# GpSimd makes the top bits of four weight halves, the first two in-projections begin in parts, and the first 30 steps get another order

## The chip, the cores and the metric

The kernel runs on one core of a Trainium2 chip. The metric is the device time of one execution in microseconds (us); lower is better. TensorE (PE) multiplies matrices, VectorE (DVE), ScalarE (ACT) and GpSimd (POOL) work elementwise, and SyncE (SP) issues nearly all DMAs. Each engine takes its instructions in the order of the program.

## The reference, cut to what matters

Chunked attention with a short window and 8 memory keys, and behind it a projection with a rational function between its two matrices:

```python
for c in range(nc):                     # 24 chunks of 32 queries, 4 batches x 8 heads, head_dim 64
    k_full = concat([mem_k, k[l_start:r_end]])        # v alike: 8 memory keys and up to 56 of the window
    a = softmax(scale * q_c @ k_full.T)
    out[c] = a @ v_full
x = out laid out as [3072, 512]
h = x @ w_in                            # w_in [512, 2048], float64 in memory
P = a0 + a1*h + a2*h**2 + a3*h**3
Q = 1 + |b0|*|h| + |b1|*h**2
return ((P / (Q + 1e-6)) @ w_out).astype(float32)     # w_out [2048, 512], float64
```

The two weight matrices are float64; the kernel gets them as pairs of 32-bit words and makes float32 of them itself.

## The kernel before, in words

The 3072 tokens are 8 blocks of 384. Attention of a block is done in 4 units (i, p): block i, head pair p. Block by block, 16 tiles j of 128 hidden features are worked through: the in-projection `g1` (12 matmuls of 384 columns: 4 slices `ct` of the contraction, each as high x high, low x high, high x low of an fp32r split), the rational function (the `chain_...` functions), and the out-projection `g2` (9 matmuls of 512 columns). One pair (i, j) is a step; `order` numbers them from 0 to 127.

In-projection n needs the four slices of x of its block, that is all four attention units, and the converted weights of its tile. Its result lies in one of two PSUM buffers `h`, which is free again for n + 2 when `chain_above` of n is done.

The first 30 steps (`HAND`) and the attention of blocks 0 to 2 are written out by hand in `SEQ`, a list of tokens; every token issues its instructions on its engines in that order, and so the string sets the order on each engine, SP's queue of DMAs too. From step 30 on a loop sets the order. The tokens, with what the prediction calls them:

- `q00`, `v00`: load of a unit's queries and keys (2 DMAs of 212 KB) and of its values (2 of 195 KB). `w`: load of one half of a weight tile (512 KB). Which half comes next is in `ORDER` (i5 is the in-half of tile 5, o5 the out-half); the tokens A, B, H, L take the halves in the same order.
- `b` scores (24 matmuls), `m` maximum and difference on DVE, `x` exponential on ACT, `c` three transposes, `k` copy of the result on ACT, `d` values (24 matmuls), `n` division on DVE, `e` three transposes back, `h` the high part of x on ACT, `l` the low part of x. For units in `XL_POOL`, `h` makes one more copy on ACT (line 432) and `l` runs on POOL (line 438), for the others on DVE (line 442).
- Conversion of a weight half: `A` (ACT, line 172) puts the rebiased high word into PSUM, `B` (DVE, two instructions, lines 177 and 178) shifts that by 3 and ors in the top 3 bits of the low word, `H` (ACT) rounds to the fp32r high part, `L` (POOL, line 190) subtracts.
- `g`: the next in-projection; `s` and `i` (ACT), `p` (POOL), `j` (DVE, `chain_above`), `t` (ACT), `r` (DVE, `chain_ratio`), `u` and `y` (POOL): its chain; `o`: the next out-projection. The prediction numbers these from 0.
- `W`: one filler transpose of the identity. `begin` issues `WARM` of them first, behind the clearing of the tiles into which q and v are loaded (`CLEAR`: tile, unit, and the engine for each half of it: v DVE, a ACT, p POOL).
- `M`: block 0's x is stored to memory. `E`: an output is moved out.

SBUF tiles are shared through slots (`QK_SLOTS`, `RAW_SLOTS`, `V_SLOTS`). q10 goes to the tile of q00 and waits until the scores b00 have read it, as q12 waits for b02; v02 lies in slot 10, v10 goes to the tile of v00.

Of the kernel before, what the change touches and what calls it, by code (L numbers as in the profile page):

```python
# [12 lines left out]
F32 = mybir.dt.float32  # L13
# [3 lines left out]
ALU = mybir.AluOpType  # L17
# [9 lines left out]
SIGN_STEP = 2.0 ** 32  # L27
W_SCALE = 2.0 ** 8
SPLIT = 10
XL_POOL = [(0, 0), (0, 1), (0, 2), (0, 3), (1, 0), (1, 1), (1, 2), (1, 3), (2, 0)]  # L30
WARM = 14
CLEAR = [("qk", 2, "va"), ("qk", 3, "pa"), ("qk", 0, "vp"), ("qk", 1, "pa"), ("v", 3, "pv"), ("v", 2, "av"), ("v", 1, "va"), ("v", 0, "ap")]
HAND = 30
BLOCKWISE = 3
BASES = {3: [30, 32, 35, 37], 4: [40, 42, 46, 50]}
# [8 lines left out]
SEQ = """
w q00 q03 q01 b00 v03 b03 m00 q02 W b01 m03 A B x00 x03 W c03 k03 w m01 W W d03 q10 b02 v01 x01 Y A c01 n03 e03 m02 w
v00 H w k01 c00 b10 h03 B x02 v02 m10 l03 d01 k00 c02 A q13 k02 x10 n01 q11 P H d00 L e01 B L w A v10 c10 d02 n00 h01
k10 H w l01 B w q12 e00 b13 n02 L b11 e02 m13 h00 A l00 m11 W d10 w h02 l02 x11 H A B c11 g k11 q21 b12 H L n10 L e10
v11 A g x13 b21 B c13 w s i B A m12 p H t j B s w d11 x12 r L c12 H g k13 v12 v13 m21 q20 n11 i w h10 j e11 k12 A L p
B t l10 s u h11 w y i p g l11 r A s w H d13 t u j i H L o n13 p x21 w B r d12 w e13 L h13 g n12 b20 y w l13 j H w A B
s L t A m20 o i B H g A H x20 u j e12 r h12 p y L L l12 v20 o s u g A B B q22 t w y c20 H r H c21 i k21 L p k20 q23 j  # L50
A A o u B t s B r g b23 L H y H i p s A L j u v21 i y m23 B M x23 o L t w g H b22 d21 j r p n21 s o A m22 L g B e21
c23 u y p i t w h21 r u s p j l21 i o k23 t g y j A H r A L u B y s g i v23 B t o H p w L r x22 u j y s H d20 d23 o
n20 t A r i w p t B j g r L s w i o u w y p g A E t o u j B w e20 s p v22 i r t j y g h20 s r H l20 p u i g j A o B
n23 g L c22 t e23 s w u p y k22 i r o t y j r s p H L H i g h23 u w A o j l23 d22 y u B o t s i A p g y r o t L j u y
s H r p n22 i t e22 B h22 u g j A H r s l22 i p L A w B A y t j B r o w u g g s i p t A L s y j o u p y H i B g r j s
t i p r H o g o u L j y B s t g E w r u y i p L o j g o s t u y H w p r L i j A B t u s p g r i H o s t j y L u A i w
r j p H L t y g B A B s p H o r u i y H g o s p u j o t g r y L u i j t y o s r i j g p o L q30 v30
"""
# [15 lines left out]
def attn_moe(ctx, tc, qk, vm, w, ab, out):  # L74
    nc = tc.nc
    P = 128
# [3 lines left out]
    TB = out.shape[0] // NBLK  # L80
# [4 lines left out]
    NCT = DM // P  # L85
# [11 lines left out]
    ps_h = ctx.enter_context(tc.tile_pool(name="ps_h", bufs=2, space=bass.MemoryType.PSUM))  # L97
# [44 lines left out]
    def half(t, kind):  # L142
        return t[:, :2 * DM] if kind == "in" else t[:, 2 * DM:]
# [50 lines left out]
    xh = {i: x_hi[i % 2] for i in range(NBLK)}  # L194
    xl = {i: x_lo[i % 2] for i in range(NBLK)}
# [559 lines left out]
```

## Time and profile before

| | us |
|---|---|
| median of 3 runs | 619.98 (618.28 to 620.85) |
| the profiled execution's own time | 619.44 |
| its span (first to last instruction) | 617.6 |
| TensorE busy | 599.1 (97%) |
| VectorE busy | 495.3 (80%) |
| ScalarE busy | 435.8 (71%) |
| GpSimd busy | 433.0 (70%) |

Busy times are shares of the span; the matmuls are pipelined, so that a group of them ends a little after the next has begun. A line of the timeline gives start, duration, engine, source line, operation, output and inputs, how many instructions are merged, and in brackets the idle time of the engine before it with what ended it. The trace of the profiled execution is what all sums below are made against; its own time is 0.54 us under the median.

### The profile page before, as it was taken

What the parts mean: (1) busy time and instruction counts of PE and PEld (TensorE: products, weight loads), DVE (VectorE), ACT (ScalarE), POOL (GpSimd) and SP (SyncE); (2) the same over time, 40 slices, a digit from 0 to 9 for tenths busy, and PEclk for the clock granted to TensorE, in tenths of its full rate; (3) what the DMA queues carried; (4) which work ended last, traced back from release to release, by engine and by line L of the source; (5) the groups of instructions that cost most, each with busy time, mean ns of one, the idle gap of its engine ahead of it and who ended that gap; (6) DMA issues with size and microseconds to landing.
All of it is one profiled execution on the core that took longest, in us unless ns stands there. A gap on an engine that the chain in (4) does not pass through costs nothing.

```text
span 617.6 us, 14151 instructions
## 1 busy us (share of the span) xinstructions
PE 599.1 (97%) x5275; PEld 528.8 (86%) x5275; DVE 495.3 (80%) x991; ACT 435.8 (71%) x822; POOL 433.0 (70%) x459
## 2 busy tenths in 40 slices
PE   6689999999999999999999999999999999999997
PEld 5568889899888888988889898888889888989996
DVE  6899998898867979788778787777878777666674
ACT  5799888798756766666667766676676766676674
POOL 2579987879966667766767676766767676776773
PEclk9999999999999999999999999999999999999999
DMA  7989437103023574342221322242122310010001
GB/s 259 359 280 360 162 110 254 48 1 146 2 83 86 177 212 146 119 133 81 82 81 38 116 68 75 81 133 82 36 62 68 101 27 14 14 51 2 0 1 51
DMA packets 42788, 64.81 MB, mean 105 GB/s; under 512 B 25696, under 2 KB 25696, under 8 KB 42336
## 3 DMA queue, kind: packets, MB, share of 16 engines
q1 hardware_dynamic: 41856, 60.61, 30.6%
q10 hardware_dynamic: 576, 1.74, 0.9%
q0 software_dynamic: 288, 1.57, 0.8%
q8 instruction: 41, 0.67, 0.4%
q14 instruction: 27, 0.22, 0.1%
HBM read 46.60 MB, written 9.44 MB: 91 GB/s over the span
## 4 chain that ended last, share of the span: by engine, by line
PE 53%; issue 18%; POOL 15%; DMA 5%; DVE 4%; ACT 2%; SPq 1%; POOLq 0%; DVEq 0%
PE o L477 25%; PE h L462 24%; POOL glo L551 6%; POOL ghi L544 6%; DMA qk<-in_qk_dram 2%; DMA w_raw<-in_w_dram 2%; POOL x_lo L440 1%; PE pairs L300 1%; POOL cy L518 1%; PE pairs L323 1%; SPq L125 1%; DMA v_main<-in_vm_dram 1%; DVE stage L177 1%; PE pa L347 1%; DVE ct L528 1%
## 5 line engine op out<-in xcount | busy, mean ns | idle before, releaser
L462 PE MATMUL h<-x_hi,w_hl 128*128 128x384 f32 x1024 | 265.1, 339 | 0.9 <-DVE ct L528 0.5
L477 PE MATMUL o<-w_hl,ghi 128*128 128x512 f32 x768 | 239.6, 393 | 0.0
L518 POOL TENSOR_TENSOR cy<-cy,ha 128x384 f32<-128x384 f32 x128 | 130.4, 1019 | 140.8 <-ACT cy L514 135.5
L462 PEld LDWEIGHTS h<-x_hi,w_hl 128*128 128x128 f32 x1024 | 185.3, 188 | 12.6 <-DVE ct L528 2.1
L462 PE MATMUL h<-x_lo,w_hl 128*128 128x384 f32 x512 | 172.5, 337 | 0.0
L477 PEld LDWEIGHTS o<-w_hl,ghi 128*128 128x128 f32 x768 | 141.8, 188 | 20.8 <-issue 0.8
L477 PE MATMUL o<-w_hl,glo 128*128 128x512 f32 x384 | 150.9, 393 | 0.0
L551 POOL TENSOR_TENSOR glo<-ct,ghi 128x384 fp32r<-128x384 f32 x127 | 129.1, 1017 | 8.9
L513 ACT ACTIVATE ha<-h 128x384 f32<-128x384 f32 x128 | 62.9, 492 | 91.7 <-PE h L462 89.4
L527 DVE TENSOR_TENSOR ct<-ct,h 128x384 f32<-128x384 f32 x128 | 70.1, 548 | 57.6 <-ACT ct L523 57.4
L544 POOL TENSOR_TENSOR ghi<-ct,zero 128x384 fp32r<-128x384 f32 x127 | 105.4, 830 | 3.8 <-DVE ct L539 2.7
L537 DVE SCALAR_TENSOR_TENSOR ct<-ct,par,cr 128x384 f32<-128x384 f32 x128 | 78.5, 613 | 33.9 <-ACT cr L533 30.9
L532 ACT ACTIVATE cr<-cy 128x384 f32<-128x384 f32 x128 | 63.2, 494 | 58.3 <-POOL cy L518 54.1
L462 PEld LDWEIGHTS h<-x_lo,w_hl 128*128 128x128 f32 x512 | 96.0, 188 | 0.0
L514 ACT ACTIVATE cy<-ha,bab 128x384 f32<-128x384 f32 x128 | 90.9, 710 | 4.5 <-DVE cr L538 0.3
L477 PEld LDWEIGHTS o<-w_hl,glo 128*128 128x128 f32 x384 | 72.0, 187 | 20.2 <-POOL glo L551 0.8
L523 ACT ACTIVATE ct<-h,par 128x384 f32<-128x384 f32 x128 | 84.1, 657 | 0.1
L528 DVE SCALAR_TENSOR_TENSOR ct<-ct,par,h 128x384 f32<-128x384 f32 x128 | 78.7, 615 | 4.5
L539 DVE SCALAR_TENSOR_TENSOR ct<-cr,ct 128x384 f32<-128x384 f32 x128 | 71.4, 558 | 4.4
L538 DVE SCALAR_TENSOR_TENSOR cr<-cy,cr 128x384 f32<-128x384 f32 x128 | 71.1, 556 | 0.4
L533 ACT ACTIVATE cr<-cr 128x384 f32<-128x384 f32 x128 | 60.8, 475 | 4.0
L190 POOL TENSOR_TENSOR w_hl<-w_raw,w_hl 128x512 fp32r<-128x512 f32 x32 | 42.1, 1316 | 6.8 <-ACT w_hl L185 6.1
(69 smaller groups left out, 406.9 us busy)
## 6 DMA issues: line engine op xcount, KB each, us to landing
w_raw<-in_w_dram SPq DMA_DIRECT2D x26, 512.0 KB, 7.0
v_main<-in_vm_dram SPq DMA_DIRECT2D x20, 390.0 KB, 4.7
qk_pairs<-in_qk_dram SPq DMA_DIRECT2D x16, 424.0 KB, 4.2
out_dram<-stage SPq DMA_DIRECT2D x24, 256.0 KB, 3.8
qk<-in_qk_dram SPq DMA_DIRECT2D x24, 212.0 KB, 4.8
v_main<-in_vm_dram SPq DMA_DIRECT2D x20, 195.0 KB, 6.0
eT<-blocks SPq DMA_DIRECT2D x80, 48.0 KB, 2.0
xf<-blocks SPq DMA_DIRECT2D x80, 48.0 KB, 2.0
```

The source lines that it names most:

```text
L462: pin(nc.tensor.matmul(h[:, :TB], lhsT=wt[:, cols], rhs=xt[i][:, ct, :], start=m == 0, stop=m == last))
L477: ins = nc.tensor.matmul(o, lhsT=gt[:, cols], rhs=wt, start=begin and m == 0, stop=end and m == 2)
L514: pin(nc.scalar.activation(c["y"], c["ha"], AF.Identity, scale=B1, bias=B0))
L518: pin(nc.gpsimd.tensor_tensor(c["y"], c["y"], c.pop("ha"), op=ALU.mult))
L523: pin(nc.scalar.activation(c["t"], c["h"], AF.Identity, scale=A3, bias=A2))
L527: pin(nc.vector.tensor_tensor(t, t, h, op=ALU.mult))
L528: pin(nc.vector.scalar_tensor_tensor(t, t, A1, h, op0=ALU.add, op1=ALU.mult))
L537: pin(nc.vector.scalar_tensor_tensor(t, t, A0, r, op0=ALU.add, op1=ALU.mult))
L538: pin(nc.vector.scalar_tensor_tensor(r, yy, QC, r, op0=ALU.add, op1=ALU.mult))
L539: pin(nc.vector.scalar_tensor_tensor(t, r, 2.0, t, op0=ALU.subtract, op1=ALU.mult, reverse0=True))
L544: pin(nc.gpsimd.tensor_tensor(ghi, chain[z]["t"], zero.broadcast_to([P, TB]), op=ALU.add))
L551: pin(engine.tensor_tensor(glo, chain.pop(z)["t"], gh[z].bitcast(F32), op=ALU.subtract))
```

## The change

The order string `SEQ` is replaced as a whole. Beside it:

```diff
-XL_POOL = [(0, 0), ..., (1, 3), (2, 0)]
+XL_POOL = [(0, 0), ..., (1, 3), (2, 1), (2, 2), (2, 3)]
-WARM = 14
-CLEAR = [("qk", 2, "va"), ("qk", 3, "pa"), ("qk", 0, "vp"), ("qk", 1, "pa"), ("v", 3, "pv"), ("v", 2, "av"), ("v", 1, "va"), ("v", 0, "ap")]
+WARM = 28
+CLEAR = [("qk", 0, "pv"), ("qk", 2, "pp"), ("v", 0, "va"), ("v", 3, "aa"), ("v", 2, "va"), ("qk", 3, "pp"), ("qk", 1, "pv"), ("v", 1, "pp")]
-ORDER = "i0 o0 i1 o1 i4 i2 i3 o3 i5 o2 i6 o4 ..."
+ORDER = "i0 i1 i2 i4 o0 i3 o1 o2 i5 i6 o3 i7 ..."
 SEQ = """
-w q00 q03 q01 b00 v03 b03 m00 q02 W b01 m03 A B x00 x03 W c03 k03 w m01 W W d03 q10 b02 v01 x01 Y A c01 n03 e03 m02 w
-v00 H w k01 c00 b10 h03 B x02 v02 m10 l03 d01 k00 c02 A q13 k02 x10 n01 q11 P H d00 L e01 B L w A v10 c10 d02 n00 h01
-k10 H w l01 B w q12 e00 b13 n02 L b11 e02 m13 h00 A l00 m11 W d10 w h02 l02 x11 H A B c11 g k11 q21 b12 H L n10 L e10
-v11 A g x13 b21 B c13 w s i B A m12 p H t j B s w d11 x12 r L c12 H g k13 v12 v13 m21 q20 n11 i w h10 j e11 k12 A L p
...
+w A q00 q03 b03 v03 q01 b00 w m03 m00 R x03 c03 x00 q10 B k03 b01 A d03 R m01 b10 q02 c00 n03 m10 B e03 x01 v01 v00
+c01 H k00 b02 Y L k01 h03 m02 d01 x10 l03 n01 x02 d00 H w e01 q11 c10 n00 A R q13 h01 c02 L e00 v02 w B l01 k02 k10
+b13 h00 H l00 b11 w d02 P m13 m11 f01 A R x11 v10 A f00 n02 c11 e02 k11 B L h02 d10 w w f10 q12 H A w l02 f11 f02 B
+x13 n10 B g A B b12 c13 H q21 v11 f12 e10 b21 w L s p m12 i A v12 t H k13 j H g s B L i p r d11 w x12 v13 g n11 j A t
...
-RAW_SLOTS = [9, 6, 9, 7, 8, 11, 13, 14, 12, 10, 12, 14, 16, 11, 15, 16]
+RAW_SLOTS = [8, 7, 5, 10, 9, 12, 13, 14, 11, 10, 11, 14, 16, 15, 15, 16]

+TOP_BITS = 4
+    def w_tops(key):                                   # token R
+        low, high = words(key)
+        tops = half(raws[key[1]], key[0]).bitcast(mybir.dt.uint16).rearrange("p (f four) -> p f four", four=4)[:, :, 1]
+        pin(nc.gpsimd.tensor_scalar(low, tops, 2.0 ** -13, 7.0, op0=ALU.mult, op1=ALU.min))
     def w_bits(key):                                   # token B
+        if done["B"] < TOP_BITS:
+            pin(nc.vector.scalar_tensor_tensor(low, fi, 3, low, op0=ALU.logical_shift_left, op1=ALU.bitwise_or))
+            return
         pin(nc.vector.tensor_scalar(fi, fi, 3, None, op0=ALU.logical_shift_left))
         pin(nc.vector.scalar_tensor_tensor(low, low, 29, fi, op0=ALU.logical_shift_right, op1=ALU.bitwise_or))
-    def g1(n):
+    def g1(n, only=None):
+        if n not in ahead:
+            ahead[n] = list(range(NCT))
+            hps[n] = ps_h.tile([P, 512], F32, name="h", tag="h")
+        left, h = ahead[n], hps[n]
+        for ct in [only] if only is not None else list(left):
+            terms = ((w_hi, xh), (w_lo, xh), (w_hi, xl))
+            for m, (wt, xt) in enumerate(terms):
+                pin(nc.tensor.matmul(..., start=len(left) == NCT and m == 0, stop=len(left) == 1 and m == len(terms) - 1))
+            left.remove(ct)
...
+        elif kind == "f":                              # token f01: step 0, slice ct 1
+            g1(i, p)
```

A token `f` does three matmuls, those of one slice, of in-projection 0 or 1; a later `g` does the slices that are left. The rounding of the top bits is new: they are scaled and converted, where they were shifted.

## Rows read from the trace of the kernel before

**Rows 1.** Windows: length, busy (count) of PE, PEld, DVE, ACT, POOL, clock, DMA share, GB/s.
```profile
0.00:5.97 5.97, 3.25 (x14) 2.88 (x15) 3.01 (x5) 5.22 (x8) 4.24 (x14) 1.00 0.63 204
5.97:32.35 26.38, 17.65 (x335) 13.30 (x336) 21.05 (x49) 15.81 (x34) 9.88 (x9) 1.00 0.95 338
32.35:44.70 12.35, 10.96 (x120) 9.10 (x120) 11.72 (x25) 11.30 (x25) 8.59 (x9) 1.00 0.81 270
44.70:60.00 15.30, 15.18 (x136) 12.66 (x137) 14.65 (x30) 14.99 (x30) 14.51 (x15) 1.00 0.97 340
60.00:80.00 20.00, 19.21 (x158) 15.80 (x157) 19.30 (x38) 16.93 (x33) 18.06 (x18) 1.00 0.57 208
80.00:617.60 537.60, 532.82 (x4516) 475.07 (x4514) 425.61 (x848) 371.53 (x697) 377.70 (x397) 1.00 0.26 78
```

**Rows 2.** Windows of line 598 alone (fillers): length, PE, PEld, clock, DMA, GB/s.
```profile
0.00:32.35 32.35, 4.56 (x19) 3.52 (x19) 1.00 0.89 313
```

**Rows 3.** Timeline of PE: the fillers, the first scores, and the waits behind them.
```profile
2.21 3.25 PE L598 MATMUL warm<-ident 128*128 128x128 f32 x14 [2.21 <-POOL ident masks.py:199]
5.97 0.86 PE L347 MATMUL pa<-qk 128*32 128x128 f32 x24 [0.51 <-DMA qk<-in_qk_dram]
7.94 0.86 PE L347 MATMUL pa<-qk 128*32 128x128 f32 x24 [1.10 <-DMA qk<-in_qk_dram]
...
22.34 0.87 PE L402 MATMUL pa<-v_first,eT 128*32 128x130 f32 x24 [0.58 <-DMA v_first<-in_vm_dram]
...
32.35 0.86 PE L347 MATMUL pa<-qk 128*32 128x128 f32 x24 [0.97 <-DMA qk<-in_qk_dram]
...
41.32 0.52 PE L425 MATMUL pa<-ident,xt 128*128 128x128 f32 x3 [0.88 <-DVE xt L415]
42.34 0.62 PE L462 MATMUL h<-x_hi,w_hl 128*128 128x384 f32 x2 [0.50 <-DVE ct L528]
```

**Rows 4.** Tile qk: clears on POOL, count, ns min/median/max, first and last start.
```profile
L217 POOL MEMSET qk<- x5: 485/485/486, 0.9 to 4.3; 128x464 f32 x5
```

**Rows 5.** Timeline of SP: DMA issues q00 q03 q01, and q10.
```profile
1.88 3.75 SPq L125 DMA_DIRECT2D qk<-in_qk_dram  x6
...
8.91 1.12 SPq L125 DMA_DIRECT2D qk<-in_qk_dram  x2
```

**Rows 6.** Timeline of DVE: the first maximum, both instructions of B, waits.
```profile
6.93 0.09 DVE L357 MEMSET pa<- 32x32 f32 x1 [2.62 <-PE pa L347]
...
10.80 0.69 DVE L178 SCALAR_TENSOR_TENSOR w_raw<-w_raw,stage 128x512 uint32<-128x512 uint32 x1
...
19.64 0.70 DVE L177 TENSOR_SCALAR stage<-stage 128x512 uint32<-128x512 uint32 x1 [0.86 <-ACT stage L172]
...
22.70 0.73 DVE L178 SCALAR_TENSOR_TENSOR w_raw<-w_raw,stage 128x512 uint32<-128x512 uint32 x1
```

**Rows 7.** Waits of DVE, 5 to 90 us: total, times, longest.
```profile
DVE pa L357 <- PE pa L347: 3.3, 2, 2.6
DVE stage L177 <- ACT stage L172: 1.9, 3, 0.9
```

**Rows 8.** DMA issues up to 32.35 us: count, KB each, median us to landing.
```profile
w_raw<-in_w_dram SPq DMA_DIRECT2D x10, 512.0 KB, 6.5
qk<-in_qk_dram SPq DMA_DIRECT2D x18, 212.0 KB, 4.8
```

**Rows 9.** Chain of waits, from 32 us: start, duration, a whole in-projection.
```profile
33.70 2.10 PE h L462 x12
```

**Rows 10.** Timeline of POOL: the first work behind the clears, and one L.
```profile
16.82 1.01 POOL L438 TENSOR_TENSOR x_lo<-xf,x_hi 128x384 fp32r<-128x384 f32 x1 [12.00 <-ACT xf L432]
...
23.72 1.31 POOL L190 TENSOR_TENSOR w_hl<-w_raw,w_hl 128x512 fp32r<-128x512 f32 x1
```

**Rows 11.** Line 442, l on DVE; line 432, the copy on ACT.
```profile
L442 DVE TENSOR_TENSOR x_lo<-pa,x_hi x3: 548/549/551, 81.3 to 126.6; 128x384 fp32r<-128x384 f32 x3
...
L432 ACT COPY xf<-pa x9: 473/484/505, 16.2 to 102.1; 128x384 f32<-128x384 f32 x9
```

More of the change, by code (lines that the diff above doesn't have):

```diff
@@ L29 @@
 SPLIT = 10
-XL_POOL = [(0, 0), (0, 1), (0, 2), (0, 3), (1, 0), (1, 1), (1, 2), (1, 3), (2, 0)]
-WARM = 14
-CLEAR = [("qk", 2, "va"), ("qk", 3, "pa"), ("qk", 0, "vp"), ("qk", 1, "pa"), ("v", 3, "pv"), ("v", 2, "av"), ("v", 1, "va"), ("v", 0, "ap")]
+XL_POOL = [(0, 0), (0, 1), (0, 2), (0, 3), (1, 0), (1, 1), (1, 2), (1, 3), (2, 1), (2, 2), (2, 3)]
+WARM = 28
+CLEAR = [("qk", 0, "pv"), ("qk", 2, "pp"), ("v", 0, "va"), ("v", 3, "aa"), ("v", 2, "va"), ("qk", 3, "pp"), ("qk", 1, "pv"), ("v", 1, "pp")]
 HAND = 30
@@ L41 @@
 XB = {"xf": 2, "eT": 2}
-ORDER = "i0 o0 i1 o1 i4 i2 i3 o3 i5 o2 i6 o4 i7 o6 i8 o5 i9 o7 o8 o9 i13 i10 o10 o13 i12 o12 i11 o11 i14 o14 i15 o15"
+ORDER = "i0 i1 i2 i4 o0 i3 o1 o2 i5 i6 o3 i7 o5 o4 i8 o6 i9 o7 o8 o9 i13 i12 o13 i10 o10 o12 i11 o11 i14 o14 i15 o15"
 V_SLOTS = [10, 11]
 SEQ = """
-w q00 q03 q01 b00 v03 b03 m00 q02 W b01 m03 A B x00 x03 W c03 k03 w m01 W W d03 q10 b02 v01 x01 Y A c01 n03 e03 m02 w
-v00 H w k01 c00 b10 h03 B x02 v02 m10 l03 d01 k00 c02 A q13 k02 x10 n01 q11 P H d00 L e01 B L w A v10 c10 d02 n00 h01
@@ L47 @@
-k10 H w l01 B w q12 e00 b13 n02 L b11 e02 m13 h00 A l00 m11 W d10 w h02 l02 x11 H A B c11 g k11 q21 b12 H L n10 L e10
-v11 A g x13 b21 B c13 w s i B A m12 p H t j B s w d11 x12 r L c12 H g k13 v12 v13 m21 q20 n11 i w h10 j e11 k12 A L p
-B t l10 s u h11 w y i p g l11 r A s w H d13 t u j i H L o n13 p x21 w B r d12 w e13 L h13 g n12 b20 y w l13 j H w A B
-s L t A m20 o i B H g A H x20 u j e12 r h12 p y L L l12 v20 o s u g A B B q22 t w y c20 H r H c21 i k21 L p k20 q23 j
-A A o u B t s B r g b23 L H y H i p s A L j u v21 i y m23 B M x23 o L t w g H b22 d21 j r p n21 s o A m22 L g B e21
@@ L52 @@
[L52 to L56, printed above, removed]
@@ L57 @@
-r j p H L t y g B A B s p H o r u i y H g o s p u j o t g r y L u i j t y o s r i j g p o L q30 v30
+w A q00 q03 b03 v03 q01 b00 w m03 m00 R x03 c03 x00 q10 B k03 b01 A d03 R m01 b10 q02 c00 n03 m10 B e03 x01 v01 v00
+c01 H k00 b02 Y L k01 h03 m02 d01 x10 l03 n01 x02 d00 H w e01 q11 c10 n00 A R q13 h01 c02 L e00 v02 w B l01 k02 k10
+b13 h00 H l00 b11 w d02 P m13 m11 f01 A R x11 v10 A f00 n02 c11 e02 k11 B L h02 d10 w w f10 q12 H A w l02 f11 f02 B
+x13 n10 B g A B b12 c13 H q21 v11 f12 e10 b21 w L s p m12 i A v12 t H k13 j H g s B L i p r d11 w x12 v13 g n11 j A t
@@ new lines @@
+w e11 s L u y L i q20 h10 g w p B h11 l11 m21 d13 c12 r H M n13 x21 j s v21 A w l10 o L k12 t w B u r p y u i H L d12
+e13 h13 l13 w A g n12 B j q23 v20 s b20 m20 H i o e12 p t x20 j A g L H r y h12 w l12 A u B g B y L t A H s L o i B H
+c20 c21 k21 k20 r L A j A o p B u g H d21 y B t w L H q22 w s i p r b23 L o H j n21 m23 u s i A L w B y g t b22 j A o
+r p H m22 L g s u x23 B y e21 t r c23 o p i H u y s j t k23 i L r g w p h21 j o l21 A A s B t u g i d20 v23 B H r n20
+w j p y x22 s H L t r p w d23 A w o i g B u j L t s w y u i p o j e20 h20 r g y n23 E u l20 s t o c22 r H e23 k22 p i
@@ L58 @@
+h23 w j t r y v22 l23 g u g A s y i p j A B o B t u L s p A H g w o i L r j s d22 t y g o B u i r j p s A y H t H u
+n22 L r p g y e22 i h22 o t L w l22 w j g o s p i u A B r j t y H r u s A i p B g t s B j y o u A H r w i y o p t w j
+g r g s L i u H y j A p L o u B t r y o s p i E t j g L s i r j u H p g y B t o g L w s r i u p H t j s o w r y i A A
+B p A g s j o L u y B g H t i u y B L H o j r p s o i j t r H u L g p y s u t i y p g r j t s o o i L u y g r p o j
+q30 v30
 """
@@ L451, in attn_moe @@
     part = [dr.tile([TB, DM], F32, name=f"part{i}") for i in range(2)]
-    def g1(n):
+    ahead = {}
+    def g1(n, only=None):
         i, j = order[n]
-        h = hps[n] = ps_h.tile([P, 512], F32, name="h", tag="h")
-        last = 3 * NCT - 1
+        if n not in ahead:
+            ahead[n] = list(range(NCT))
+            hps[n] = ps_h.tile([P, 512], F32, name="h", tag="h")
+        left, h = ahead[n], hps[n]
         w_hi, w_lo = whi("in", j), wlo("in", j)
-        m = 0
-        for ct in range(NCT):
+        for ct in [only] if only is not None else list(left):
             cols = slice(ct * P, (ct + 1) * P)
-            for wt, xt in ((w_hi, xh), (w_lo, xh), (w_hi, xl)):
-                pin(nc.tensor.matmul(h[:, :TB], lhsT=wt[:, cols], rhs=xt[i][:, ct, :], start=m == 0, stop=m == last))
-                m += 1
+            terms = ((w_hi, xh), (w_lo, xh), (w_hi, xl))
+            for m, (wt, xt) in enumerate(terms):
+                pin(nc.tensor.matmul(h[:, :TB], lhsT=wt[:, cols], rhs=xt[i][:, ct, :], start=len(left) == NCT and m == 0,
+                                     stop=len(left) == 1 and m == len(terms) - 1))
+            left.remove(ct)
     def g2(n):
@@ L553, in attn_moe @@
     w_seq = [({"i": "in", "o": "out"}[x[0]], int(x[1:])) for x in ORDER.split()]
-    done = dict.fromkeys("wABHL", 0)
+    done = dict.fromkeys("wRABHL", 0)
     last = {i: max(n for n, (m, j) in enumerate(order) if m == i) for i in range(NBLK)}
@@ L620, in attn_moe @@
     single = dict(g=g1, s=chain_abs, p=chain_below, i=chain_line, j=chain_above, t=chain_inverse, r=chain_ratio, u=chain_hi, y=chain_lo, o=g2)
-    convert = dict(w=lambda key: w_load(*key), A=w_abs, B=w_bits, H=w_hi, L=w_lo)
+    convert = dict(w=lambda key: w_load(*key), R=w_tops, A=w_abs, B=w_bits, H=w_hi, L=w_lo)
     def hand(token):
```

## The prediction

> **What bounds the kernel now.** I read first how busy each engine is by stretch [rows 1]. From 80 us on TensorE works 532.82 of 537.60 us, and step 30 and all behind it are left as they are; so the end comes as much sooner as TensorE reaches that stretch sooner. What can be won is TensorE's lost time ahead of it: idle time, and fillers that compute nothing. Up to 32.35 us (where the scores b12 begin) it is busy 3.25 + 17.65 = 20.90 us, of which 4.56 are fillers [rows 2], so its real work is 16.34 us and 32.35 - 16.34 = 16.01 us are lost. From there to 80 us the idle time is 1.39 + 0.12 + 0.79 = 2.30 us. TensorE's timeline then says what its waits end on [rows 3]: loads of queries and keys early, the last of them 0.97 us for q12 at 32.35, and later DVE (0.88 and 0.50 us). Behind these stand two others. The 16 DMA engines are busy 95% from 6 to 32 us, and DVE works 45.67 of the 47.65 us from 32.35 to 80 (11.72 + 14.65 + 19.30). So the loads set the first 32 us, and TensorE and DVE run close together up to 80.
>
> **The start.** 14 fillers took 3.25 us from 2.21 on, and the first scores followed at 5.97 [rows 3]. 28 take 6.5, which ends at some 8.6 (the last one's run through the array counts once). Scores b03 now stand first. q03 was the second load and landed for the scores at 7.94; now q00 can go at once, but q03's two clears are fourth and fifth on GpSimd, some 0.92 + 0.29 + 5 x 0.45 = 3.5 us (0.485 each, overlapping [rows 4]), against an issue at 1.88 + 1.25 = 3.1 before [rows 5]. It lands by 8.3, under the fillers. So b03 runs at 8.6 and b00 ends at 8.6 + 2 x 0.8 = 10.2 instead of 6.8. DVE's first maximum moves from 6.93 [rows 6] to 9.5. But DVE had waited 3.3 us in two parts for the first two scores [rows 7], 2.62 and so 0.7, and the second part falls away now: it is some 1.8 us behind, not 2.5.
>
> **The loads up to q12.** I counted the transfers ahead of q12 in both strings: 7 halves of weights, 7 pairs of q loads, 5 of v loads, the same in both, another order within. With the DMA engines at 95% q12 lands where it did, unless they run dry. Two new stops in SP's queue could do that. q10 goes into the tile of q00 and so waits for b00. SP has issued all ahead of it by 7.7 us (six DMAs took 3.75 us, so 0.62 each [rows 5]), and b00 ends at 10.2: a stop of 2.5 us, with q02, v01, v00, the loads i2 and q11 to q12 queued behind it; before, q10 went at 8.91 with no stop. The load i3 goes to slot 10, where v02 lies, and waits for the values d02, which read v02. v02 was there at 22.34 [rows 3]; it now has 0.35 MB more ahead of it, 1.0 us at 338 GB/s [rows 1], and with 0.5 of dry time (below) it lands near 24, so that d02 ends near 25.4, behind b11. SP would be there at 22.1 (20 DMAs at 0.6 behind 10.2): 3.3 us, with o1, q12 and q21 behind. Loads landed 4.8 us (q) to 6.5 us (w) after their issue [rows 8], against some 3.4 for q00 ahead of the crowd (its second half issued near 2.5, its scores at 5.97 [rows 3, 5]); so 1.4 to 3.1 us of work stand in the queue and cover most of a stop. I take 0.5 us of dry time for both (between 0, all covered, and 5.8, nothing covered; nearest to the cover). A gain is bounded by the 5% of idle DMA time, 1.3 us.
>
> **The parts.** By b12 both orders have given TensorE the same scores, transposes and values and one in-projection. The new one has in addition f10 and f11: 6 matmuls at 2.10 / 12 us [rows 9] = 1.05 us, and no fillers of the five W. At an equal landing of q12 the lost time is 16.01 - 1.05 = 14.96. f01 and f00 fill idle time too, but it ends on q12 all the same: step 0's in-projection, that I put at 30.3 where it ended 0.97 us ahead of 32.35 [rows 3], has b12 behind it on TensorE. So of some 2.1 us that the four parts fill, 1.05 count.
>
> **GpSimd's new work.** Four R. The trace has no such instruction. Bounds: a clear of 464 elements at 0.49 [rows 4] below, the two-input subtraction of 512 at 1.31 [rows 10] above; not below nothing, as it is work added. I take 1.1, near the upper row, since input and output are converted. The first two fall into 12.00 us in which GpSimd did nothing [rows 10] and cost nothing. The third and fourth wait for the loads i2 and i4 (some 20.8 and 25.6 us by the same count of bytes) and have l01, l00 and l02 behind them. l02 then ends near 29.7, and f02 with the rest of g0 behind it at 30.3, under q12. If R took 1.3 more, that cover is gone and TensorE loses about 0.5. Three units of block 2 go to GpSimd and one comes back: two more l (2 x 1.01 [rows 10]) and two copies on ACT (2 x 0.48 [rows 11]), all past 60 us; I cost them at nothing, as GpSimd has 1.94 us free of 20 there and ACT 3.07 [rows 1].
>
> **DVE's relief.** Four first instructions of B go, 4 x 0.70 = 2.8 us [rows 6], and 2 x 0.55 of l [rows 11]. Against this stand the later start, 1.8 us, and waits that I find for b10 (q10 is out at 11.5 and 3.4 later lands near 15: 1.1 us) and for q13 and i2 (1.6 us), where before there were 1.9 in three waits for a conversion [rows 7]: 0.8 more. Net DVE is 2.8 - 1.8 - 0.8 = 0.2 us ahead from 33 us on and 1.3 past the l. Following both orders along with these durations, its j and r of steps 0 to 8 come 0 to 2 us sooner, the tight ones (j of step 1, before g of step 3, which was the 0.50 us wait at 42.34 [rows 3]) 1.3 us sooner.
>
> A row beside this: B's second instruction took 0.73 us at 22.70, with L on GpSimd ahead and behind it, and 0.69 at 10.80, where GpSimd did nothing [rows 6, 10]. The Trainium skill's page "GPSIMD Engine Reference", section 1 (Specifications), says that GpSimd shares its SBUF interfaces with VectorE and contends with DVE instructions of two SBUF inputs or a 2-port mode, which speaks against giving GpSimd DVE's work. If DVE stood still for all of the four R, an estimate by that page, 4.4 us would go and more than the 2.8 won; by the row it is 0.04 an instruction, and that is what I take.
>
> **Sum.** 1.05 (parts) - 0.5 (dry DMA) + 0.9 (of the 2.30 us idle behind 32.35, what a DVE ahead by 0 to 2 us saves) = 1.45 us. Made against the profiled execution: 619.44 - 1.5 = 617.9. The median stands 0.54 higher: **618.4**. Bounds of the same terms: 1.05 + 1.3 + 2.30 = 4.65 (615.3), and 1.05 - 5.8 = -4.75 (624.7).
>
> **Rivals.**
> 1. All waits behind 32.35 go, and the DMA engines don't run dry: 1.05 + 2.30 to 4.65 = 3.4 to 4.65, about 616.3. For it: DVE has 3.9 us less in all. Against: it begins late and has no idle time to catch up.
> 2. DVE cancels it: 1.8 us later start and 2.7 us of early waits eat the 2.8 and TensorE is held at the same j and r as before: what the parts give is spent in waits for `ct`; 619.9. For it: DVE's 26.37 of 27.65 us between 32.35 and 60 [rows 1]. Against: the j's that decide come sooner by my sums.
> 3. The slower side: the stops at q10 and i3 come through. Every us past the cover delays q12, and TensorE stands at b12. From 32.35 + 1.05 + 2.3 = 35.7 us for b12 on the kernel is surely slower; with both stops in full, b12 at 38.1, less the 2.3 that the later idle time may give back, it is 2.4 to 4.7 us slower: 623.3. For it: SP's queue is in order. Against: the backlog of 1.4 to 3.1 us.
> 4. The clock. The five W go, and TensorE waits for loads from 13 to 25 us. The granted clock was 1.00, so 2.4 GHz, in all stretches, the one from 5.97 to 32.35 with 17.65 of 26.38 us busy among them [rows 1]. At 1.2 GHz the scores, values and parts on the way to g0 would take twice as long, 2 to 3 us of which half lies under loads: 621. The Trainium skill's "TensorE: Matmul & The Clock Gate", Part 1, says that the throttled state is the default and activity releases it; by that rule gaps between the scores cost, and the trace so far shows none that did.
>
> **Chances.** Forecast 0.44 (its own range 617.2 to 619.6), rival 1 0.29, rival 2 0.12, rival 3 0.12, rival 4 0.03. A measurement of this kernel can tell about 0.5%, 3.1 us, from no change: faster is under 616.9, slower over 623.1. Faster: 0.23 of rival 1 and 0.05 of the forecast, 0.28. Slower: 0.08 of rival 3 and 0.02 of the others, 0.10. Same: 0.62. The range takes in rival 1 to 614.8 and rival 3 to 622.8.
>
> **What would show it.** First scores near 8.6 us; SP waiting some 2.5 us for b00 ahead of q10 and some 3 us for d02 ahead of i3; DMA share still 0.93 or more from 5 to 30 us; b12 at 32.3 to 33.0 with TensorE waiting there for q12; TensorE's later waits, up to 80 us, near 1.4 us; R between 0.5 and 1.3 us; clock 1.00. I am wrong if b12 runs before 31 or after 34.5, if waits for `ct` or `xt` beyond 3 us stand between 33 and 80 us, or if R takes over 2 us.

## The result and the profile after

The changed kernel is slower: 624.39 us (median of 17 runs, 620.42 to 625.7) against 619.22 us for the kernel before in the same runs (618.28 to 620.85), ratio 1.0063 with an interval of 1.0051 to 1.0076. 618.4 was forecast and 622.8 was the upper end of the range. The medians are 5.2 us apart, the ratio stands for 3.9 us: the changed kernel's runs spread over 5 us. So the prices below, which are differences of medians from several rounds, are good to about 1 us. Three of all the runs below took 0.97 to 1.49 ms and are left out of the ratios. The profiled execution took 625.46 us, its span is 623.7 us, 6.1 more than before.

The windows of the changed kernel, in the columns of [rows 1]:

```profile
0.00:8.14 8.14, 5.93 (x29) 5.76 (x29) 2.31 (x4) 4.89 (x6) 7.46 (x18) 1.00 0.71 232
8.14:32.35 24.21, 16.79 (x327) 13.36 (x327) 15.09 (x39) 12.90 (x29) 12.92 (x10) 0.93 0.83 262
32.35:38.35 6.00, 2.04 (x12) 1.70 (x11) 4.16 (x8) 4.42 (x8) 2.78 (x3) 1.00 0.98 344
38.35:44.70 6.35, 6.35 (x86) 4.92 (x87) 4.67 (x10) 4.08 (x8) 1.77 (x2) 0.73 0.73 271
```

Two columns differ from [rows 1]: up to 32.35 us the DMA share is 0.83 where it was 0.95, and the granted clock is 0.93 and later 0.73 where it was 1.00. TensorE's timeline, with the waits:

```profile
2.21 6.00 PE L613 MATMUL warm<-ident 128*128 128x128 f32 x28 [2.21 <-POOL ident masks.py:199]
8.14 1.52 PE L357 MATMUL pa<-qk 128*32 128x128 f32 x48
25.50 2.79 PE L357 MATMUL pa<-qk 128*32 128x128 f32 x48 [3.92 <-ACT eT L401]
38.35 1.38 PE L357 MATMUL pa<-qk 128*32 128x128 f32 x24 [3.96 <-DMA qk<-in_qk_dram]
67.75 0.55 PE L394 MATMUL pa<-ident,e 128*128 128x128 f32 x3 [0.34 <-DVE w_raw L188]
84.77 0.52 PE L394 MATMUL pa<-ident,e 128*128 128x128 f32 x3 [0.19 <-DVE w_raw L188]
```

Two waits of 3.9 us stand out. The one ahead of 25.50 holds the scores b13 and b11; the one ahead of 38.35 is b12, 6.0 us later than in [rows 3]. Behind each the same matmuls take longer: 48 score matmuls 2.79 us at 25.50 for 1.52 at 8.14, and the 24 of b12 1.38 for 0.86 [rows 3]. The windows around them (TensorE's clock is the third number from the right):

```profile
24.00:26.00 2.00, 0.50 (x12) 0.53 (x16) 0.67 (x1) 2.00 (x6) 1.92 (x2) 0.72 0.72 266
26.00:28.00 2.00, 2.00 (x44) 2.00 (x40) 0.77 (x4) 1.24 (x4) 2.00 (x3) 0.50 0.94 318
40.00:42.00 2.00, 2.00 (x9) 1.67 (x7) 1.93 (x4) 0.97 (x3) 0.12 (x1) 0.51 0.92 301
```

0.50 is 1.2 GHz; in both places TensorE had stood idle for 3.9 us just before. The last two lines of the timeline are marks for all that follows: three transposes that wait for a weight conversion. In the trace of before they stand here:

```profile
61.79 0.52 PE L384 MATMUL pa<-ident,e 128*128 128x128 f32 x3 [0.34 <-DVE w_raw L178]
78.80 0.52 PE L384 MATMUL pa<-ident,e 128*128 128x128 f32 x3 [0.24 <-DVE w_raw L178]
```

They come 5.96 and 5.97 us later, and the span is 6.1 longer; b12 was 6.00 late already, so that the loss stands at 38.35 us and hardly changes behind it. By kind it is 1.44 us of fillers (6.00 against 4.56 [rows 2]), 1.9 us of idle TensorE (623.7 - 603.3 = 20.4 against 617.6 - 599.1 = 18.5), and the rest, 2.8 us, matmuls that take longer.

SP's timeline shows where it begins (the gap between the end of a line and the next start is SP standing still):

```profile
6.75 0.58 SPq L127 DMA_DIRECT2D w_raw<-in_w_dram  x1
9.72 2.40 SPq L127 DMA_DIRECT2D qk<-in_qk_dram  x4
16.07 0.43 SPq L127 DMA_DIRECT2D w_raw<-in_w_dram  x1
23.84 1.11 SPq L127 DMA_DIRECT2D v_main<-in_vm_dram  x2
29.09 0.81 SPq L127 DMA_DIRECT2D w_raw<-in_w_dram  x2
```

The chain of waits ties these together (start, length, what):

```profile
16.07 7.18 DMA w_raw<-in_w_dram
...
24.67 0.77 ACT eT L401 x2
25.45 0.05 issue
25.50 2.79 PE pa L357 x48
28.29 0.78 PE pa L412 x21
29.09 0.33 SPq L127
...
30.46 7.76 DMA qk<-in_qk_dram
```

SP stops 2.4 us for b00 ahead of q10 (7.33 to 9.72), and the load i2 behind it goes at 16.07 and lands at 23.25. On ACT the conversion A of i2 stands ahead of four small copies, and one of these gives b13 its PSUM tile:

```profile
23.27 0.62 ACT L174 ACTIVATE stage<-w_raw 128x512 f32<-128x512 f32 x1 [3.35 <-DMA w_raw<-in_w_dram]
24.56 0.87 ACT L401 COPY eT<-pa 128x384 f32<-128x384 f32 x2
```

So b13 is late, at the half clock, and d02 behind it too; i3, which waits for d02, stops SP for 4.1 us (24.95 to 29.09), and q12 behind i3 lands at 38.22. In the chain of the kernel before the same load stands so:

```profile
24.52 7.70 DMA qk<-in_qk_dram
```

It is issued 5.94 us later now (30.46) and lands 6.00 us later: nothing of the delay was covered.

### The profile page after: what moved, and what is told of

Read it like the earlier page. It is cut to its first block, busy times and chain, and to the rows that moved or that the text cites. A ratio compares the mean times of both kernels' runs of the same rounds, so it can differ in the third digit from the quotient of the medians.

```text
span 623.7 us, 14188 instructions
## 1 busy us (share of the span) xinstructions
PE 603.3 (97%) x5284; PEld 533.8 (86%) x5284; DVE 491.2 (79%) x984; ACT 436.0 (70%) x822; POOL 444.1 (71%) x468
## 4 chain that ended last, share of the span: by engine, by line
PE 36%; issue 29%; POOL 23%; DMA 5%; DVE 3%; ACT 2%; SPq 2%; POOLq 0%; ACTq 0%
PE o L492 16%; PE h L476 15%; POOL ghi L559 10%; POOL glo L566 9%; DMA qk<-in_qk_dram 3%; POOL x_lo L450 3%; DMA w_raw<-in_w_dram 2%; POOL cy L533 2%; SPq L127 2%; PE pa L357 1%; PE warm L613 1%; PE pa L412 1%; PE pairs L310 1%; PE pairs L333 0%; DVE ct L552 0%
```

## The experiments

All 17 are in one table. The mark is the start of the transposes that stand at 78.80 us in the trace of before; the ratio is to the kernel before, in runs beside it. A mark is of one trace, and a trace is not always near the median: e2's is of its slowest run (622.38 us), e11's of its second slowest (621.68 us).

| run | median us | ratio (interval) | mark |
|---|---|---|---|
| the change | 624.39 | 1.0063 (1.0051 to 1.0076) | 84.77 |
| e1, v02 in another slot | 622.7 | 1.0047 (1.0028 to 1.0066) | 82.41 |
| e2, q10 with a tile of its own | 620.68 | 1.001 (0.9997 to 1.0023) | 81.38 |
| e3, no R | 622.38 | 1.0042 (1.0027 to 1.0056) | 82.94 |
| e4, fillers in both waits | 621.96 | 1.0039 (1.0026 to 1.0052) | 80.61 |
| e5 = e1 + e2 | 619.85 | 1.0002 (0.9993 to 1.0011) | 78.68 |
| e6 = e5, A of i2 behind the copies | 619.94 | 1.0007 (0.9998 to 1.0016) | 78.97 |
| e7, 14 fillers at the start | 622.34 | 1.0038 (1.0025 to 1.005) | 80.00 |
| e8, before + two R | 619.99 | 1.0007 (0.9999 to 1.0016) | 79.34 |
| e9 = e5 + early start | 619.45 | 0.9997 (0.9985 to 1.0009) | 79.71 |
| e10 = e5, two R | 619.34 | 0.9994 (0.9983 to 1.0005) | 79.33 |
| e11 = e5, no parts | 620.12 | 1.0009 (0.9996 to 1.0023) | 80.98 |
| e12 = e9 + e10 | 619.55 | 0.9993 (0.9981 to 1.0006) | 78.90 |
| e13 = e12, q12 sooner | 620.39 | 1.0001 (0.9989 to 1.0014) | 79.55 |
| e14 = e13, o1 converted later | 622.34 | 1.0035 (1.0023 to 1.0048) | 81.69 |
| e15 = e5, less DVE work late | 620.33 | 1.0001 (0.9992 to 1.001) | 79.69 |
| e16, before, less DVE work early | 620.16 | 0.9999 (0.999 to 1.0009) | 79.07 |
| e17, before, less DVE work late | 619.58 | 0.9991 (0.9978 to 1.0003) | 78.20 |

### Which part makes it slower: e1 to e4

e1 takes the second stop away, e2 the first, e3 GpSimd's R (DVE does both instructions of B again), e4 leaves all stops and gives TensorE work to do in both waits.

```diff
e1 -V_SLOTS = [10, 11]
e1 +V_SLOTS = [6, 11]
e2 -QK_SLOTS = {..., 1: [12, 13, 14, 15], ...}
e2 +QK_SLOTS = {..., 1: [16, 13, 14, 15], ...}
e3 -TOP_BITS = 4
e3 +TOP_BITS = 0                    # and w_tops returns at once
e4 -b13 h00 H l00 b11 ...
e4 +W W W W W W W W W W W W W W b13 h00 H l00 b11 ...
e4 +        for _ in range(16 if (i, p) == (1, 2) else 0):      # ahead of the scores b12
e4 +            pin(nc.tensor.transpose(out=s[:, :P], in_=ident, identity=ident))
```

> v02 lies in slot 6 instead of 10, so that the load i3 has no wait for the values d02. Theory A (the loads behind SP's stops make scores b12 late, and the waits also drop the clock): i3 goes right behind v10, near 25 us instead of 29.1; q12 lands some 4 us sooner, b12 runs near 34.3 instead of 38.35, where the rest of in-projection 0 ends, and the second fall of the clock goes: 4 to 5.5 us less than the changed kernel, 619 to 620.5. Theory B (the 2.0 us top-bit instructions on GpSimd, which DVE waits for, cost the time): no change, 624.

> Block 1's first unit gets slot 16, so that q10 does not wait until the scores b00 have read q00. Theory A: q10 goes at 7.4 instead of 9.7 us, all loads behind it some 2 us sooner, i2 lands at 21 instead of 23.3, b13 starts at 23 instead of 25.5, d02 and with it i3 and q12 2 us sooner; b12 at 36; 2 to 3.5 us less than the changed kernel, 621 to 622.5. Theory B: i2's top bits start 2 us sooner too, but the other three cost what they did: under 1 us less.

> No top bits on GpSimd: B has its two instructions for all halves, as before the change. Theory A: b12 runs at 38.3 as before, since q12 sets it; DVE has 2.8 us more to do, part of it under its waits: no change to 1.5 us slower, 624 to 626. Theory B: 2 to 4 us less, 620.5 to 622.

> 14 filler transposes ahead of scores b13 and 16 ahead of b12, into PSUM that the scores then overwrite, so that TensorE works where it waits. Theory A: the clock stays at 1.00, b13 still starts near 25.5 and b12 near 37, what was run at 0.5 behind both waits (some 2.8 us for b13 and b11, 3.7 for b12 to b21) takes half: 2.5 to 3.5 us less, 621 to 622, and the runs lie closer together. Theory B: no change, 624, as nothing on GpSimd or DVE moves.

With q10's own tile (e2) the scores b13 wait 0.70 us, at full clock, and 3.7 us come back. TensorE of e2:

```profile
23.11 1.52 PE L357 MATMUL pa<-qk 128*32 128x128 f32 x48 [0.70 <-ACT eT L401]
35.47 0.86 PE L357 MATMUL pa<-qk 128*32 128x128 f32 x24 [2.21 <-DMA qk<-in_qk_dram]
```

With v02 elsewhere (e1) b12 does not wait any more, but b13 does, and the half clock stays; 1.7 us come back. TensorE of e1:

```profile
24.91 2.79 PE L357 MATMUL pa<-qk 128*32 128x128 f32 x48 [3.47 <-DMA qk<-in_qk_dram]
```

So the first stop is the one that matters more. In e1 ACT's copies were done at 23.81 and b13 still waited, for the load q13: the first stop reaches b13 by two ways, ACT's queue and q13 itself, and no run separates them. R alone is not the cause: without it (e3) the kernel is still 0.4% slower, and e5 below keeps all four R and is even with the kernel before. But e3 takes 2.0 us off where none were expected, and why R costs that much while the stops are in stays open. The fillers (e4) leave both stops in, and the clock is whole from 16 us on. TensorE of e4:

```profile
22.06 1.69 PE L615 MATMUL warm<-ident 128*128 128x128 f32 x14
23.85 1.52 PE L359 MATMUL pa<-qk 128*32 128x128 f32 x48
...
34.69 0.86 PE L359 MATMUL pa<-qk 128*32 128x128 f32 x24 [0.43 <-DMA qk<-in_qk_dram]
```

b12 comes at 34.69 instead of 38.35, and in the median 2.4 us come back; that is the price of the clock that the waits bring down, as far as this run shows it. The trace alone would make it too large: its 28 fillers at the start took 4.74 us for 6.00, so that q10 went at 8.82 for 9.72, and b13 starts 1.65 us sooner although the clock up to there was no higher. The runs of the changed kernel itself point the same way: the three with a mean clock of 1.000 took 620.42, 620.8 and 621.89 us, the ten at 0.994 or less 623.6 to 625.7. The two go together there, which is no test, and a whole clock is not all of it: e4's eight runs at 1.000 took 621.23 to 624.14 us.

Two of the four expectations missed: e1 was to take 4 to 5.5 us off, and e3 none. e2 took slightly more than the 2 to 3.5 us expected, e4 slightly less than its 2.5 to 3.5.

### Both stops gone: e5, e6 and e7

```diff
e5, e6 +V_SLOTS = [6, 11]
e5, e6 +QK_SLOTS = {..., 1: [16, 13, 14, 15], ...}
e6 -... n00 A R q13 ... v02 w B l01 k02 k10 / b13 h00 H l00 ...
e6 +... n00 R q13 ... v02 w l01 k02 k10 / b13 h00 A B H l00 ...
e7 -WARM = 28
e7 +WARM = 14                       # the stops stay
```

> Both: v02 in slot 6 and q10 in a tile of its own (slot 16), so that neither stop in SP's queue is left. Theory A (the stops, by late loads and the clock that falls in the waits): what the two gave alone adds up where both were on the path, -1.7 and -3.7 us from 624.4, at most 619.0; b12 by 33.5, no clock below 1.00 up to 45 us. Theory C (the late first scores and the 2.0 us top bits cost the rest, the loads only part): 620 to 621, no better than q10's tile alone.

> As the one with neither stop, and on ScalarE the conversion A of half i2, which waits for its load, stands behind h01, k02, k10 and h00 instead of ahead of them. Theory A: b13 no longer waits for the copies behind A; it starts as soon as q13 has landed, near 22; d02 by 25, b12 by 33; 618.5, equal to the kernel before or under it. Theory C: 620 to 621.

> WARM back to 14, all else as changed. Theory A: the first scores wait for q03, near 7.5 instead of 8.1; q10's stop ends 0.6 us sooner and DVE starts 0.6 us sooner; 0.5 to 1 us less, 623.5 to 624. Theory C: the late start is a main cost, and the fillers gone give 2 us: 622. If the fillers hold the clock up, it falls in the waits ahead of c03 and the time goes up instead: over 625.

Two slot numbers bring back all of the loss: e5 is the kernel before in time, 619.85. It does not matter then where A of i2 stands on ACT (e6). The theory that the stops are all had put both lower, at 619.0 or less and at 618.5. Half the fillers with the stops left in (e7) ends the first stop sooner (q10 goes at 8.89 for 9.72), shortens b13's wait to 1.39 us and gets 2 us back, where 0.5 to 1 were expected. TensorE of e7 at b12:

```profile
33.55 1.51 PE L357 MATMUL pa<-qk 128*32 128x128 f32 x24 [2.23 <-DMA qk<-in_qk_dram]
```

These scores ran at the half clock (0.50 from 34 to 36 us) behind a wait of 2.23 us; those of e2 above took 0.86 us behind 2.21. So the length of a wait does not say alone whether the clock falls. TensorE of e5:

```profile
32.54 0.86 PE L357 MATMUL pa<-qk 128*32 128x128 f32 x24 [1.06 <-DMA qk<-in_qk_dram]
41.37 0.59 PE L476 MATMUL h<-x_hi,w_hl 128*128 128x384 f32 x2 [0.59 <-ACT cr L548]
61.74 0.55 PE L394 MATMUL pa<-ident,e 128*128 128x128 f32 x3 [0.32 <-DVE w_raw L188]
```

Its windows:

```profile
0.00:32.35 32.35, 23.52 (x364) 19.55 (x364) 20.05 (x49) 20.34 (x39) 22.59 (x29) 1.00 0.90 303
32.35:80.00 47.65, 44.61 (x407) 36.77 (x408) 45.89 (x92) 43.63 (x86) 41.80 (x40) 1.00 0.80 285
```

b12 is where it was, and ahead of it stand 23.52 - 6.11 of fillers = 17.41 us of real work against 16.34: the 1.07 us of the parts are there. But from 32.35 to 80 us TensorE is idle for 3.04 us against 2.30, and the transposes at 61.79 and 78.80 come at 61.74 and 78.68. In these two traces the gain is made and given back; by the runs, e5's interval (0.9993 to 1.0011) leaves room for a gain of 0.4 us, not for 1.05.

### What takes the gain back: e8 to e17

e8 gives the kernel before only R, for its first two halves. Of the others e9 to e15 start from e5, e16 and e17 from the kernel before: e9 lets the scores b00 and their maximum go first and halves the fillers, e10 keeps R for two halves only, e11 leaves out the parts, e12 is e9 and e10 together, e13 issues q12 ahead of i3, e14 also converts o1 only behind step 0's j. e15 to e17 leave out the first DVE instruction of B for four halves (their shift is not computed): the 9th to the 12th, behind 41 us, in e15 and e17, the first four, up to 22 us, in e16.

```diff
e9  +w A q00 q03 b00 m00 b03 v03 q01 w m03 R x00 x03 c03 q10 ...     # WARM = 14
e10 +        if done["R"] >= TOP_BITS: return                       # TOP_BITS = 2
e11  without the tokens f01, f00, f10, f11, f02, f12
e13 -... h02 d10 w w f10 q12 H A w l02 ...
e13 +... h02 d10 q12 w w f10 H A w l02 ...
e14 -x13 n10 B g A B b12 ... m12 i A v12 t H k13 j H g s B L
e14 +x13 n10 B g b12 ... m12 i v12 t H k13 j A B A H g s B L
e15, e17 +        if not 8 <= done["B"] < 12:                       # e16: 0 <= ... < 4
             pin(nc.vector.tensor_scalar(fi, fi, 3, None, op0=ALU.logical_shift_left))
```

> The kernel before, with the top bits on GpSimd for its first two halves alone (i0 and o0), placed in GpSimd's 12 us of idle time; order, slots and parts as before. Theory A: DVE has 2 x 0.70 us less to do ahead of 16 us, where it waits for loads anyway: no change, 619.0 to 619.6. Theory C: the 2.0 us instructions slow what stands around them: 620 or more. If DVE's work is what binds: 1.4 us less, 618.

> Neither stop in SP's queue (v02 in slot 6, q10 in slot 16), WARM back to 14 and scores b00 and maximum m00 ahead of b03. Theory D (with the stops gone TensorE reaches b12 with 1 us more done, and then waits for DVE, that begins at 9.1 us instead of 6.9): DVE's first maximum runs near 6.7, its j and r of steps 0 to 3 come 0.5 to 1 us sooner, 0.5 to 1 us less than with the stops gone alone: 619.0. Theory E (loads alone set DVE too, since m12 stands ahead of j of step 0 and waits for q12): no change, 619.8.

> Neither stop, and the top bits on GpSimd for two halves instead of four. The third and fourth made DVE wait 1.04 and 1.09 us for GpSimd (each takes 2.0 us behind its load, where ScalarE's A takes 0.6). Theory D: these waits go, 1.4 us of work come back, DVE is 0.7 us ahead at 33 us: 619.2 to 619.6. Theory E: no change, 619.8. If DVE's whole work binds: 1.4 us more, 621.

> Neither stop, and in-projections 0 and 1 each as a whole at their g. Theories D and E: what the parts had ready at b12 (1.05 us) was given back in waits for DVE and ScalarE by 55 us, so their loss costs little: 619.8 to 620.4. If the parts count in full: 1.05 us more, 620.9.

> All that looks good: neither stop, 14 fillers with b00 and m00 first, top bits for two halves, the parts kept. Theory D: 1 to 1.7 us less than with the stops gone alone, 618.1 to 618.9, under the kernel before. Theory E: 619.8, as the loads up to q12 are the same.

> The best one (neither stop, 14 fillers, b00 first, two top bits), and q12 ahead of the halves i3 and o1 in SP's queue. Theory E: q12 lands 2.5 us sooner, b12 runs near 30.5, when g of step 0 is done; 1 to 2 us less: 617.5 to 618.5, under the kernel before. Theory D: b12 sooner, but B of i3 and o1, whose loads are 1.1 us later, stand ahead of m12 on DVE: no change, 619.5.

> As the last, and A and B of half o1, that is needed 15 us later, stand behind j of step 0 instead of ahead of m12. Theory E: as the last or 0.3 us less. Theory D: m12 and j of step 0 come 1 to 2 us sooner, r of step 0 no sooner; 0.5 to 1.5 us less than the last.

> The kernel without the two stops, and the first instruction of B left out for the halves 9 to 12 (they stood at 41.15, 47.32, 51.20 and 57.61 us; 4 x 0.69 = 2.8 us of DVE; the shift of these halves is not computed). Theory (from 42 us on DVE sets the time, and so the 1.07 us that the parts gave at b12 were given back): the transposes that waited for a conversion at 61.74 come 1 to 1.5 us sooner, bounded by TensorE's idle time from 42 to 80 us (0.81 + 0.47 + 0.22 = 1.5); 618.4, ratio to before 0.998. Rival (loads or TensorE itself set it): they stay at 61.7, 619.8, ratio 1.000.

> The kernel before with the first instruction of B left out for the halves 1 to 4 (10.08, 15.13, 19.64, 21.98 us; 2.8 us of DVE; the shift of these halves is not computed): the relief of the change alone, without GpSimd's work and without the new order. Theory (DVE has 9.6 us of idle time ahead of 61 us, nearly all ahead of 32, where it waits for loads): the relief turns into idle time, the transposes at 61.79 come 0 to 0.4 us sooner, 619.2, ratio 0.9995. Rival (DVE's whole work counts wherever it goes): 1.2 us sooner, 618.0, ratio 0.998.

> The kernel before with the first instruction of B left out for the halves 9 to 12 (42.20, 47.28, 52.27, 54.87 us; 2.8 us of DVE; the shift of these halves is not computed). Theory: DVE bounds the stretch from 42 to 80 us, so the transposes at 61.79 come sooner by TensorE's idle time there, 0.50 + 0.34 and a little behind, at most 1.25; 618.2, ratio 0.998. Rival (TensorE is the bound there): at 61.5 at the soonest, 619.2, ratio 1.000.

None is measurably faster than the kernel before; the lowest ratios, those of e17, e12 and e10, are within their intervals of no change. e8 and e16 price DVE's relief by itself: with R for two halves the mark is at 79.34, and with 2.8 us of DVE work simply left out of the first four conversions at 79.07, both no sooner than 78.80. The clock fell in both traces (to 0.66 from 20 to 24 us in e8, to 0.63 from 28 to 32 in e16), so the ratios count for more, and both intervals hold no change. DVE's windows up to 61.7 us (length, busy time and count, clock, DMA), before:

```profile
0.00:61.70 61.70, 52.10 (x110) 1.00 0.90 314
```

and e5:

```profile
0.00:61.70 61.70, 48.22 (x105) 1.00 0.88 305
```

Both have by then 14 conversions, 10 maxima, 8 divisions and 5 of j behind them. DVE works 3.9 us less and is idle 3.9 us more, so the relief has become waits: those of the maxima of blocks 0 and 2 for their scores grew from 3.3 to 6.3 us in all (nearly all of it the start), and 2.1 us are waits for R, in the place of 1.9 for ACT [rows 7].

e13 takes the wait at b12 away and moves it: DVE gets to j of step 0 later, since i3's conversion now waits ahead of it. DVE of e13:

```profile
31.68 0.70 DVE L189 TENSOR_SCALAR stage<-stage 128x512 uint32<-128x512 uint32 x1 [1.24 <-ACT stage L174]
36.44 0.61 DVE L545 SCALAR_TENSOR_TENSOR ct<-ct,par,h 128x384 f32<-128x384 f32 x1
```

In e5 that j stood at 35.54. e14 brings it back to 35.46 and loses more behind it: ratio 1.0035, and in its trace the clock is at 0.50 from 36 to 40 us.

e15 and e17 tested the thought that DVE alone sets the stretch from 42 us on. It fell. With 2.8 us of DVE work gone the transposes at 61.79 do not wait any more, but the next engine does the holding. TensorE of e15:

```profile
33.69 0.86 PE L358 MATMUL pa<-qk 128*32 128x128 f32 x24 [1.60 <-DMA qk<-in_qk_dram]
69.38 0.50 PE L493 MATMUL o<-w_hl,ghi 128*128 128x512 f32 x1 [0.58 <-POOL w_hl L201]
79.69 0.52 PE L395 MATMUL pa<-ident,e 128*128 128x128 f32 x3 [0.20 <-DVE w_raw L189]
```

and of e17:

```profile
31.12 0.86 PE L348 MATMUL pa<-qk 128*32 128x128 f32 x24
41.77 0.62 PE L463 MATMUL h<-x_hi,w_hl 128*128 128x384 f32 x2 [0.50 <-DVE ct L529]
61.95 0.50 PE L478 MATMUL o<-w_hl,glo 128*128 128x512 f32 x1 [0.29 <-POOL glo L552]
69.42 0.58 PE L463 MATMUL h<-x_hi,w_hl 128*128 128x384 f32 x2 [0.30 <-ACT cy L515]
78.20 0.52 PE L385 MATMUL pa<-ident,e 128*128 128x128 f32 x3 [0.28 <-DVE w_raw L179]
```

The marks, 0.6 us sooner in e17 and 1.0 later in e15, are not the edits' doing: both edits begin behind 41 us, and b12 stands at 33.69 in e15 for 32.54 in e5, and at 31.12 in e17 for 32.35 in the kernel before. Traces of the same instructions lie up to 1.2 us apart there, so that marks closer than this tell nothing alone. Counted from a point that the edit does not reach, e15 takes 46.00 us from b12 to the mark and e5 46.14; e17 takes 36.43 from 41.77, and the kernel before 36.46 from 42.34 [rows 3]. So 2.8 us of DVE work were worth 0.03 to 0.14 us. Of the 1.07 us that e5 leads by at 32.35 us in these traces, 0.84 are lost by 50 us (idle there 2.35 against 1.51 us), in five waits of 0.2 to 0.6 us for q21, DVE, ACT and a conversion. Which of these would have to go first is open; each that was taken away let another come. The gains expected of e9, e12, e13, e14, e15 and e17, 0.5 to 2 us each, did not show; e8, e10, e11 and e16 came out near no change, as their first theories had it.

## Why the prediction was wrong, step by step

**What bounds the kernel.** The loads set the first 32 us, as said. That TensorE and DVE run close together up to 80 us is half of it: GpSimd and ACT are as close there (e15, e17).

**The start.** First scores at 8.14 (8.6 said), DVE's first maximum at 9.10 (9.5 said).

**The loads: the step that failed.** "So 1.4 to 3.1 us of work stand in the queue and cover most of a stop. I take 0.5 us of dry time for both." The stops themselves were foreseen: 2.4 us for q10 (2.5 said), 4.1 for i3 (3.3 said). The cover was not there: the DMA share was 0.83, not 0.93 or more, and b12 came at 38.35, where the prediction's full price of both stops had 38.1. Rival 3 is what happened, and it had 0.12. Two things were wrong in the step. The cover was worked out from the median time to landing, 4.8 to 6.5 us, and taken once for two stops; q12 itself took 7.70 us to land before and 7.76 now, so that its landing moved as far as its issue. And only q12 was followed behind the stops; the first stop's price went another way, over the load i2 and ACT's queue, or q13, to b13, d02 and so into the second stop. Of the 5.2 us, e2 takes 3.7 back alone, e1 1.7, both 4.5: they are not independent.

**The clock.** Rival 4, with 0.03, came as a consequence of rival 3, and so on top of it. The prediction had argued that the clock held at 1.00 over 17.65 busy of 26.38 us; what this trace adds is that it falls to 0.50 behind single waits of 3.9 us. One trace of the kernel before was too few to tell that it holds there: e17, the same up to 41 us, has it at 0.62 and 0.52 from 20 to 24 us. The Trainium skill's "TensorE: Matmul & The Clock Gate", Part 1, says that throttled is the default and activity lifts it; the trace agrees, with 2.79 us for 48 matmuls that take 1.52 at full clock. By e4 the fillers that held the clock were worth some 2.4 us.

**The parts.** 1.05 said, 1.07 in e5, and not to be seen in the time: with and without them e5 and e11 are within their intervals, though without them e11's trace has TensorE idle for 4.05 us up to 28.60.

**R.** 1.1 us said, with 1.31 as the upper bound. It takes 2.0, over the bound: two rows of GpSimd,

```profile
6.20 2.00 POOL L179 TENSOR_SCALAR w_raw<-w_raw 128x512 uint32<-128x512 uint16 x1
23.32 1.97 POOL L179 TENSOR_SCALAR w_raw<-w_raw 128x512 uint32<-128x512 uint16 x1 [4.79 <-DMA w_raw<-in_w_dram]
```

and DVE waits for the one that begins late:

```profile
25.33 0.69 DVE L185 SCALAR_TENSOR_TENSOR w_raw<-stage,w_raw 128x512 uint32<-128x512 uint32 x1 [4.36 <-POOL w_raw L179]
```

That the two-input subtraction is dearer than anything with one input was an assumption; here the one-input instruction reads every fourth 16-bit word and writes every second 32-bit one, and converts. Which of these costs the time was not tested.

**DVE's relief.** "Net DVE is 0.2 us ahead" was right in kind: e5's j of step 0 is at 35.54 (35.29 before) and that of step 1 at 40.62, 1.05 sooner (1.3 said). The 0.9 us that this was to save did not come: TensorE's wait ahead of in-projection 3 is 0.59 us in e5 where it was 0.50, and another engine ends it. B's one instruction took 0.69 us at 25.33 and 30.76 with GpSimd at work beside it, and 0.68 and 0.70 at 11.55 and 16.36 without; in e5 it took 0.73 and 0.70 against 0.68 twice. So nothing of the 4.4 us showed. The Trainium skill's "GPSIMD Engine Reference", section 1, names DVE instructions with two SBUF inputs or in a 2-port mode; B reads one of its inputs from PSUM (`stage`), so it has not two SBUF inputs, and these rows do not test what is stated there. Once the stops are gone, rival 2 has the time (619.9), and its mechanism in part: the early waits did eat the relief, but j of step 1 came sooner and another engine held TensorE.

## What to carry to other kernels

When a buffer is reused by a load in one queue, the price of the stop is what every load behind it then does, on each engine that has that load's consumer standing in order ahead of other work; follow each of them, not only the one that was late before. The backlog in the DMA queue was no cover here: two slot numbers were worth 4.5 us. Work taken from an engine in a stretch where it waits for loads was worth nothing (e16), and where four engines run within 5% of each other (44.70 to 60 us [rows 1]), 2.8 us taken from one of them were worth 0.03 us (e17). Compare two traces from a point that the edit does not reach: up to there the same instructions lay up to 1.2 us apart.

## What the runs showed of the hardware

A wait can cost TensorE twice: behind 3.9 us of idle time it ran at a granted clock of 0.50, and filler transposes put into the waits (1.69 us for the first 14, at a clock of 1.00) made the whole kernel 2.4 us faster than without them. Shorter waits went either way: 24 score matmuls took 1.51 us behind 2.23 us (e7) and 0.86 behind 2.21 (e2). GpSimd's strided, converting instruction took 2.0 us for 512 elements a partition, four times the 0.49 of a clear of 464 [rows 4].
